# Top-32 selection on halves of the keys, and MLP work paced by the steps left

## The chip, the cores and the metric

The kernel runs on one core of a Trainium2 chip, in fp32. The metric is the device time of one execution in microseconds. PE is the matrix engine, DVE the vector engine, ACT the scalar engine, POOL is GpSimd, SP issues most of the DMAs.

## The reference

Attention over the 32 best keys, and then an MLP block on its output. Cut to what matters:

```python
# q, k, v: batch 8, heads 8, sequence 576, head_dim 64
scores = scale * np.matmul(q, k.transpose(0, 1, 3, 2))
kth = np.partition(scores, -32, axis=-1)[..., -32:-31]
scores = np.where(scores >= kth, scores, -1e9)
scores = scores - scores.max(-1, keepdims=True)
attn = np.exp(scores); attn = attn / (attn.sum(-1, keepdims=True) + 1e-9)
x = (attn @ v) as (8, 576, 512)                      # heads side by side
xn = (x - mean) / np.sqrt(var + 1e-6) * g_ln         # over the 512 columns
out = x + np.maximum(xn @ w_ch1, 0) @ w_ch2          # 512 -> 2048 -> 512
```

## The kernel before, in words

The work is cut into *units*. A whole unit is 128 queries of two heads (a head pair, `hp`); its scores are two tiles of 128 rows and 576 keys. The 64 queries that are left of each head pair form a *rest unit*: both heads in one tile. There are 160 units: 128 whole and 32 rest. Units are grouped into *jobs* (a batch, a head pair and some query tiles); batch 0 goes through query tiles 0 and 1 for all four head pairs, then 2 and 3, then the rests; later batches go through 0 and 1 and then 2 and 3, and the rests are added to the second part in batch 1 and to the first part from batch 2 on.

The main loop runs over steps n, and step n is named after the unit whose selection falls in it. Each engine works through its instructions in the order in which the loop emits them, so one step holds pieces of several units:

- PE and ACT: `scores(n+1)`, matmuls into PSUM (L347) and ACT copies of 288 columns into the tile `sc` (L328);
- DVE: `select(n, 0..3)` at four places of the step. It finds the 32nd largest score of each row: four times MAX8 (the eight largest of a row, L364), with three MATCH_REPLACE8 between them that overwrite these eight by a very low number (L369; each comes with a short MATCH_VALUE_LOAD). All of them run over 576 columns. The first reads `sc`, the others the scratch `wk`;
- ACT and POOL: `prepare(n-1)` computes the bias of the exponential (from unit 16 on POOL does, L390 and L391), `mask(n-1)` writes e from sc and the threshold (L394), and `weigh` takes the exponential of unit n-2 (L404);
- PE and ACT: `turn` transposes the weights of unit n-2 (L457, L490). For some whole units (`moved`, 84 in all) one tile goes another way instead: a DVE transpose (L434) and DMAs;
- PE: `values` multiplies a finished group of units with v (L515, L522), `place` transposes the output back (L554);
- DVE: `turn_heads` transposes k and q of a coming job (L300), `stats` computes mean and variance of finished rows (L581, L582), after which POOL subtracts the mean (L583).

In the first steps (up to 15) ACT, POOL and DVE also convert the 32 pieces of the weights w1 and w2, which arrive as 64-bit numbers (`weights`, L178 to L197).

The MLP runs on PE in the gaps. When two row tiles of a batch are finished (three where the rests of two batches are added), they become a `Block`; at a fixed step `give` puts its work into the list `todo`: transposes of x (L611), 64 `hidden` matmuls (L624) and 16 `project` matmuls a tile (L641). Blocks are given at steps 9, 19, 31, 44 (three tiles), 55, 63, 76 (three), 83, 95, 103, 116 (three), 123, 135, 143, 156 (three) and 163. `fill`, called at eight places of a step, takes items from `todo` as long as their costs are covered by what is `owed`; each call adds an eighth of what the planner allows the step (but no more than 6 us in all may be owed):

```python
DVE_UNIT, DVE_REST, DVE_MOVE = 10.3, 5.3, 0.8
def slot(n):
    return max(0.0, dve_cost(n) - pe_cost(n)) / SLOTS
```

`dve_cost` and `pe_cost` are the planner's own estimates for the step without MLP, in us. What remains in `todo` after the last step is run off at once.

In the code shown here, `halve` and what belongs to it are not yet there.

Of the kernel before, what the change touches and what calls it, by code (L numbers as in the profile page):

```python
# [10 lines left out]
ALU = mybir.AluOpType  # L11
FP32 = mybir.dt.float32
U32 = mybir.dt.uint32
PSUM = bass.MemoryType.PSUM

TOP_K = 32
LOWEST = -3.0e38
# [11 lines left out]
def kernel(  # L29
# [41 lines left out]
    nc = tc.nc  # L71
    P = nc.NUM_PARTITIONS
    B, H, S, D = q.shape
    DM = H * D
    DFF = w_ch2.shape[0]
    NC, NF = DM // P, DFF // P
# [8 lines left out]
    def pool(name, bufs, **kw):  # L85
        return ctx.enter_context(tc.tile_pool(name=name, bufs=bufs, **kw))
# [3 lines left out]
    HALF = S // 2  # L90
# [3 lines left out]
    kqpool = pool("kq", 4)  # L94
    vpool = pool("v", NV)
    scpool = pool("sc", 4)
    wpool = pool("wk", 2)
    epool = pool("e", 3)
    ptpool = pool("pt", 1)
    otpool = pool("ot", 2)  # L100
    restpool = pool("ot_rest", 1)
    small = pool("small", 4)
# [6 lines left out]
    hbmpool = pool("hbm", 4, space=bass.MemoryType.DRAM)  # L109
    psps = pool("ps", 5, space=PSUM)  # L110
    mmps = pool("mmps", 3, space=PSUM)

    def const(shape, name):
        return consts.tile(shape, FP32, tag=name, name=name)
# [20 lines left out]
    w2 = const([P, NF, DM], "w2")  # L135
# [4 lines left out]
    class Piece:  # L140
# [22 lines left out]
        def fetch(self):  # L163
            self.raw = xpool.tile([P, DM, 2], U32, tag="x", name="raw")
            nc.sync.dma_start(self.raw[:].rearrange("p n w -> p (n w)"), self.src)

        def split(self):
# [3 lines left out]
            high = self.raw[:, :, 1].bitcast(FP32)  # L171
            self.size = tmp("size", U32)
            self.low = tmp("low", FP32)
# [16 lines left out]
        def join(self):  # L190
            size = self.size[:]
            nc.gpsimd.tensor_tensor(size, size, self.low[:].bitcast(U32), ALU.add)
            size = size.bitcast(FP32)
# [42 lines left out]
    todo = []  # L236
    stores = []
    share = [0.0]
# [65 lines left out]
    class Unit:  # L304
        def __init__(self, job, group, qt):
            self.job, self.group, self.qt = job, group, qt
            self.rest = qt == J
            self.tiles = [(0, 1)] if self.rest else [(0,), (1,)]

            self.moved = False  # L310
            self.weighed = 0

    class Group:
# [18 lines left out]
    def score_half(u, s):  # L332
# [20 lines left out]
                    )  # L353
        return pss

    def select(u, i):

        nt = range(len(u.tiles))
        if i == 0:
            u.cur = [u.sc[:, t] for t in nt]  # L360
            u.wk = {}
        m = small.tile([P, 2, 8], FP32, tag=f"m{i}", name=f"m{i}")
        for t in nt:
            nc.vector.max(m[:, t, :], u.cur[t])  # L364
        if i < TOP_K // 8 - 1:
            for t in nt:
                if i == 0:
                    u.wk[t] = wpool.tile([P, S], FP32, tag="wk", name="wk")
                nc.vector.match_replace(u.wk[t][:], m[:, t, :], u.cur[t], LOWEST)  # L369
                u.cur[t] = u.wk[t][:]  # L370
        if i == 0:
            u.top = m
        u.thr = m
# [321 lines left out]
    units = []  # L695
# [8 lines left out]
    END = N + 6  # L704
# [9 lines left out]

    CONVERTING = max(n for n in batches if batches[n]) + 2
    EARLY = jobs[NHP].first
    for u in units[CONVERTING:]:
        u.moved = not u.rest and u is not u.group.units[-1]

# [2 lines left out]
    gives = {}  # L722
# [8 lines left out]
    for j in jobs:  # L731
        if j.hp == NHP - 1:
            b = j.b
            step = j.last + (3 if j.last < EARLY else 4)
            tiles = [(b, qt) for g in j.groups for qt in g.qts if qt < J]
# [17 lines left out]
    SLOTS = 8  # L753
# [4 lines left out]
    def after(n):  # L758

        turned = at(n - 1) if n - 1 < EARLY else at(n - 2) if n - 2 >= EARLY else None  # L760
        last = at(n - 2) if n - 2 < EARLY else at(n - 3) if n - 3 >= EARLY else None
        return turned, last.group if last and last is last.group.units[-1] else None

    DVE_UNIT, DVE_REST, DVE_MOVE = 10.3, 5.3, 0.8


    turns = {}
# [4 lines left out]
    def pe_cost(n):  # L772
        c = 0.0
        if at(n + 1):
            c += 1.25 if at(n + 1).rest else 1.5
        ex, g = after(n)
        if ex:
            c += 0.67 if ex.rest else 0.55 if ex.moved else 1.0
        if g:
            c += 0.6 + 7.8e-3 * g.nq  # L780
        return c

    def dve_cost(n):
        u, ex = at(n), after(n)[0]
        c = 5.0 if u is None else DVE_REST if u.rest else DVE_UNIT
        return c + DVE_MOVE if ex and ex.moved else c

    def give(n):
# [8 lines left out]

    def slot(n):

        return max(0.0, dve_cost(n) - pe_cost(n)) / SLOTS  # L800

    recips, rows_of = {}, {}

# [18 lines left out]
    for n in range(END):  # L822
        now[0] = n
        if n in gives:
            give(n)
        share[0] = slot(n)
        u, nxt, mk = at(n), at(n + 1), at(n - 1)
        ex, g = after(n)
        g = g if g and not g.quick else None
        late = at(n - 4)  # L830
        late = late if late and late.rest and late.job.b % 2 else None
        parts = turn(ex) if ex else []
        early = ex is not None and n - 1 < EARLY
        last = ex and ex is ex.group.units[-1]
        quick = ex.group if last and ex.group.quick else None

        moved = ex is not None and ex.moved
        order = (1, 0) if moved else (0, 1)
        sent, stores[:] = stores[:], []

        if ex and not early:
            weigh(ex, order[0])
        if nxt:
            scores(nxt)
        if g:
            values(g)
        if u:
            select(u, 0)
        if moved:
            move(ex)  # L850
        for store in sent:
            store()
        for den in recips.pop(n, []):
            nc.vector.reciprocal(den, den)
        if n == gives_first:
            for blk, i in rows_of.pop(n):
                blk.stats(i)
        if mk:
            prepare(mk)
        if early:  # L860
            for t in range(2):
                mask(ex, t)
                weigh(ex, t)
        if not quick:
            weights(n, 0)
        fill()
        if ex and len(ex.tiles) > 1 and not early:
            weigh(ex, order[1])
        fill()
        if parts and not moved:  # L870
            parts[0]()
        if ex and ex.rest:
            keep_den(ex)
        if u:
            select(u, 1)
        if n in turns:
            turn_heads(turns[n])
            later = fresh.index(turns[n]) + 1
            if later < len(fresh):
                load(fresh[later], nc.sync, nc.sync)  # L880
        for blk, i in rows_of.pop(n, []):
            blk.stats(i)
        for blk in gives.get(n - 1, []):
            blk.std()
        if not quick:
            weights(n, 1)
        fill()
        if mk and not early:
            mask(mk, int(mk.moved))
        if g:  # L890
            place(g)
        if late:
            place_rest(late.job.b, late.job.hp)
        fill(1 if g or late else 0)
        fill()
        if moved:
            parts[0]()
        elif len(parts) > 2:
            parts[1]()
        if u:  # L900
            select(u, 2)
        for blk in gives.get(n - 2, []):
            blk.inverse()
        if last and ex.group.sums is not None:
            recips.setdefault(n + 1, []).append(ex.group.sums)
        last_rest = at(n - 3)
        if last_rest and last_rest.rest and last_rest.job.b % 2:
            hp = last_rest.job.hp
            den = dr[last_rest.job.b // 2][:, 2 * hp : 2 * hp + 2]
            recips.setdefault(n + 1, []).append(den)  # L910
        fill()
        if parts:
            parts[-1]()
        if mk and len(mk.tiles) > 1 and not early:
            mask(mk, 1 - int(mk.moved))
        fill()
        for x in (u if n < EARLY else None, mk if n > EARLY else None):
            if x and x is units[x.job.last]:
                load_values(x.job)
        if quick:  # L920

            values(quick)
            for den in recips.pop(n + 1):
                nc.vector.reciprocal(den, den)
            place(quick)
            weights(n, 0)
            weights(n, 1)
        if u:
            select(u, 3)
        for x in (g, quick):  # L930
            if x and x.job.hp == NHP - 1:
                for qt in x.qts:
                    if qt < J:
                        arrived(n, (x.job.b, qt), xs[x.job.b, qt])
        if late and late.job.hp == NHP - 1:
            r = late.job.b // 2
            arrived(n, ("r", r), rs[r])
        fill()
# [37 lines left out]
```

## Time and profile before

| | |
|---|---|
| Median of 15 runs | 1751.93 us (1749.52 to 1755.8) |
| The profiled execution | 1750.6 us, of which its span is 1748.8 us |
| Mean granted PE clock | 0.962 of full speed |
| Busy time | PE 1616.1, DVE 1547.8, ACT 1117.1, POOL 287.7 us |
| Selection on DVE | MAX8 1152 instructions, 814.4 us; MATCH_REPLACE8 864 instructions, 635.7 us |
| MLP on PE | hidden 547.9 us, project 532.8 us of modelled busy time |
| Last unit's selection starts | 1612.1 us |

Busy time on PE is modelled: the records of matmuls that follow one another overlap, so their pitch, from start to start, tells more than their length. The same holds a little for DVE: a MAX8 record lasts 0.74 us, but the next one starts 0.66 us after it. In a row of the trace the first number is the start in us from the span's start, then comes the duration, the engine, the line, the operation, and the tiles written and read with their shapes; "x2" merges two instructions. A row of the groups ends with the busy time, the mean in ns of one, and the idle time of the engine before it with what ended it. In the page's slices each digit is a fortieth of the span, 43.7 us.

### The profile page before, as it was taken

To read this page: it belongs to the slowest core of one execution; us is meant where nothing else is said; L and a number is where in the kernel's file an instruction comes from. 1 tells how busy PE (TensorE), PEld (TensorE's weight loads), DVE (VectorE), ACT (ScalarE), POOL (GpSimd) and SP (SyncE) were. 2 spreads that over 40 slices of the span, in tenths; PEclk is the share of its full clock that TensorE was granted. 3 is DMA by queue.
4 is the path that set the end of the run, shared out by engine and by line. 5 is a ranking of instruction groups with operands and counts; after the bars stand their busy time and mean duration, and the time that the engine had idled before them with its cause. 6 is when DMAs were issued, how large, how long until landed. Compare 5 with 4: busy or idle time off the path is not lost.

```text
span 1748.8 us, 23687 instructions
## 1 busy us (share of the span) xinstructions
PE 1616.1 (92%) x7065; PEld 972.7 (56%) x7065; DVE 1547.8 (89%) x3228; ACT 1117.1 (64%) x2842; POOL 287.7 (16%) x513
## 2 busy tenths in 40 slices
PE   4559899799699999999999999999999999998998
PEld 2337466475355575745547575745547575745564
DVE  7987999989989999999999999999999999999100
ACT  7767876656565766666666676666656667667310
POOL 5664510010100101010110101010110101001000
PEclk9669999889799999999999999999999999999999
DMA  7432233112321133212322132212322132111000
GB/s 177 116 91 67 70 63 69 56 44 70 77 57 50 51 77 78 56 50 58 77 69 56 45 72 75 64 50 58 70 74 59 45 72 69 51 56 45 19 18 13
DMA packets 309832, 110.79 MB, mean 63 GB/s; under 512 B 247236, under 2 KB 290248, under 8 KB 309704
## 3 DMA queue, kind: packets, MB, share of 16 engines
q1 hardware_dynamic: 304968, 108.68, 24.4%
q10 hardware_dynamic: 4736, 0.59, 0.3%
q8 instruction: 57, 0.93, 0.2%
q14 instruction: 71, 0.58, 0.1%
HBM read 77.73 MB, written 31.46 MB: 62 GB/s over the span
## 4 chain that ended last, share of the span: by engine, by line
PE 69%; DVE 13%; ACT 8%; issue 7%; POOL 2%; DMA 1%; POOLq 0%; ACTq 0%; SPq 0%; DVEq 0%
PE hps L624 26%; PE ops L641 19%; PE scps L347 9%; PE av L515 7%; DVE m L364 6%; DVE wk L369 5%; PE tp L457 4%; PE av L522 2%; ACT e L404 2%; ACT e L394 1%; PE tp L611 1%; PE xo L554 1%; ACT size L178 1%; ACT sc L328 1%; POOL x L583 1%
## 5 line engine op out<-in xcount | busy, mean ns | idle before, releaser
L364 DVE MAX8 m<-wk 128x8 f32<-128x576 f32 x864 | 611.0, 744 | 2.0
L624 PE MATMUL hps<-xT,w 128*128 128x256 f32 (+1 forms) x2048 | 547.9, 414 | 6.5 <-ACT xT L616 4.0
L641 PE MATMUL ops<-w,h 128*128 128x512 f32 x1152 | 532.8, 596 | 0.0
L624 PEld LDWEIGHTS hps<-xT,w 128*128 128x128 f32 x2048 | 379.6, 193 | 111.9 <-issue 19.7
L369 DVE MATCH_REPLACE8 wk<-m,wk 128x576 f32<-128x576 f32 x576 | 423.8, 743 | 0.0
L641 PEld LDWEIGHTS ops<-w,h 128*128 128x128 f32 x1152 | 203.6, 190 | 196.5 <-issue 192.9
L347 PE MATMUL scps<-kT,qT 64*128 64x288 f32 (+3 forms) x1344 | 245.4, 444 | 32.0 <-DVE qT L300 14.7
L328 ACT COPY sc<-scps 128x288 f32<-128x288 f32 x576 | 197.8, 418 | 56.0 <-PE scps L347 42.3
L404 ACT ACTIVATE e<-e,bias 128x576 f32<-128x576 f32 x288 | 226.7, 787 | 0.8
L394 ACT ACTIVATE e<-sc,m 128x576 f32<-128x576 f32 x288 | 224.4, 779 | 1.6 <-DVE m L364 0.8
L347 PEld LDWEIGHTS scps<-kT,qT 64*128 64x128 f32 (+1 forms) x1344 | 136.6, 183 | 145.6 <-issue 49.2
L369 DVE MATCH_REPLACE8 wk<-m,sc 128x576 f32<-128x576 f32 x288 | 211.9, 743 | 0.0
L364 DVE MAX8 m<-sc 128x8 f32<-128x576 f32 x288 | 203.4, 743 | 6.9 <-ACT sc L328 6.9
L636 ACT ACTIVATE h<-hps 128x256 f32<-128x256 f32 (+1 forms) x256 | 105.5, 413 | 161.2 <-PE hps L624 159.7
L457 PE MATMUL tp<-ident,e 128*128 128x128 f32 x816 | 132.8, 288 | 47.9 <-ACT e L404 47.7
L457 PEld LDWEIGHTS tp<-ident,e 128*128 128x128 f32 x816 | 103.2, 147 | 121.7 <-ACT e L404 70.6
L390 POOL TENSOR_TENSOR bias<-m,m 128x2 f32<-128x2 f32 (+1 forms) x144 | 28.1, 195 | 832.2 <-DVE m L364 763.3
L515 PE MATMUL av<-pt,vb 128*64 128x256 f32 (+2 forms) x1088 | 149.8, 418 | 3.0 <-DMA vb<-in_v_dram 2.8
L515 PEld LDWEIGHTS av<-pt,vb 128*64 128x64 f32 x1088 | 75.1, 144 | 72.1 <-issue 24.7
L469 ACT COPY pt<-tp 128x512 f32<-128x512 f32 x128 | 75.5, 590 | 55.8 <-PE tp L457 55.3
L527 ACT COPY oT<-av 128x256 f32<-128x256 f32 (+2 forms) x68 | 26.3, 387 | 116.7 <-PE av L522 116.7
L434 DVE STREAM_TRANSPOSE sc<-e 128x512 f32<-128x512 f32 x84 | 59.3, 705 | 40.0 <-ACT e L404 40.0
(70 smaller groups left out, 1096.7 us busy)
## 6 DMA issues: line engine op xcount, KB each, us to landing
turned<-sc SPq DMA_DIRECT2D x84, 256.0 KB, 2.0
pt<-turned SPq DMA_DIRECT2D x336, 64.0 KB, 2.0
vb<-in_v_dram SPq DMA_DIRECT2D x136, 128.0 KB, 2.5
raw<-in_moe_w_ch_dram SPq DMA_DIRECT2D x32, 512.0 KB, 4.1
kin<-in_k_dram SPq DMA_DIRECT2D x128, 72.0 KB, 2.4
qin<-in_q_dram SPq DMA_DIRECT2D x120, 72.0 KB, 2.5
out_dram<-o SPq DMA_DIRECT2D x32, 256.0 KB, 2.2
ends<-in_v_dram SPq DMA_DIRECT2D x136, 16.0 KB, 2.3
```

The costliest lines, as they stand in the source:

```text
L328: nc.scalar.copy(u.sc[:, t, s * HALF : (s + 1) * HALF], made[s][t][:, 0:HALF])
L347: nc.tensor.matmul(ps[i * R : i * R + ql, o : o + width], qT[r, q0 : q0 + ql], kT[r, k0 : k0 + width], start=True, stop=True,)
L364: nc.vector.max(m[:, t, :], u.cur[t])
L369: nc.vector.match_replace(u.wk[t][:], m[:, t, :], u.cur[t], LOWEST)
L394: nc.scalar.activation(u.e[:, t], u.sc[:, t], AF.Prelu, bias=u.thr[:, t, 7:8], scale=-1.0, alpha=SLOPE)
L404: nc.scalar.activation(u.e[:, t], u.e[:, t], AF.Exp, bias=u.bias[:, t : t + 1], scale=-scale / SLOPE, accum_out=g.den[:, col : col + 1],)
L457: nc.tensor.transpose(ps[:, c * P : (c + 1) * P], u.e[:, t, c * P + t * R : (c + 1) * P + t * R], ident[:],)
L469: nc.scalar.copy(g.pt[:, 0:J, q0 : q0 + P], ps[:].rearrange("p (c n) -> p c n", n=P))
L515: nc.tensor.matmul(av[h * D : (h + 1) * D, 0 : g.nq], vb[:, h * J + c, :], g.ptB[:, 0 : g.nq // 32, c, :] if h else g.pt[:, c, 0 : g.nq], ...
L624: nc.tensor.matmul(ps["h"][:, 0:N], w1[:, c, f * P : (f + 1) * P], xT[0][:, c, 0:N], start=(c == 0), stop=(c == NC - 1),)
L636: nc.scalar.activation(hT[f], ps["h"][:, 0:N], AF.Relu)
L641: nc.tensor.matmul(ps["o"][:], hT[f][:, i * P : (i + 1) * P], w2[:, f, :], start=(f == 0), stop=(f == NF - 1),)
```

## The change

From unit 8 on (`EARLY`), the selection works on halves of the keys. The 576 scores of a row are taken as 288 pairs (column j with column 288 + j). DVE writes the larger of each pair into a new tile `hi`. GpSimd computes the smaller one from the bits, as integers: it adds both scores into `lo` and, once `hi` is there, subtracts it, which leaves exactly the other one's bits. At most 16 of the 32 largest scores can be smaller ones of their pair. So `select_halved` takes the 16 largest of `lo` (two MAX8 and one MATCH_REPLACE8 over 288 columns) and writes them into 16 columns behind the 288 of `hi`; then the four MAX8 and three MATCH_REPLACE8 follow over the 304 columns of `hi`. `halve(n+1)` is emitted in step n after `select(n, 1)`.

The first 8 units keep the old selection; their scratch is now the last part of the tile `w2`, which isn't filled yet at that time. The pool `wk` goes; `hi` (two buffers), `lo` (one) come in its place, and the pool `e` has two buffers instead of three.

In the planner a halved unit's cost on DVE counts 0.9 of what it did. After step 16 a step is allowed the larger of two: the old difference of DVE and PE costs, and the cost of all that is in `todo` divided by the number of steps to the next block plus two.

```diff
-    wpool = pool("wk", 2)
-    epool = pool("e", 3)
+    hipool = pool("hi", 2)
+    lopool = pool("lo", 1)
+    epool = pool("e", 2)
...
+    def halve(u):
+        nt = len(u.tiles)
+        u.lo = lopool.tile([P, 2, HALF], FP32, tag="lo", name="lo")
+        u.hi = hipool.tile([P, 2, HALF + TOP_K // 2], FP32, tag="hi", name="hi")
+        a, b = u.sc[:, 0:nt, 0:HALF], u.sc[:, 0:nt, HALF:S]
+        lo, hi = u.lo[:, 0:nt], u.hi[:, 0:nt, 0:HALF]
+        nc.gpsimd.tensor_tensor(lo.bitcast(I32), a.bitcast(I32), b.bitcast(I32), ALU.add)
+        nc.vector.tensor_tensor(hi, a, b, ALU.max)
+        nc.gpsimd.tensor_tensor(
+            lo.bitcast(I32), lo.bitcast(I32), hi.bitcast(I32), ALU.subtract
+        )
+
+    def select_halved(u, i):
+        nt = range(len(u.tiles))
+        def replace(m, t, x):
+            nc.vector.match_replace(x[:, t], m[:, t, :], x[:, t], LOWEST)
+        if i == 0:
+            for o in range(HALF, HALF + TOP_K // 2, 8):
+                for t in nt:
+                    nc.vector.max(u.hi[:, t, o : o + 8], u.lo[:, t])
+                if o == HALF:
+                    for t in nt:
+                        replace(u.hi[:, :, o : o + 8], t, u.lo)
+            return
+        for r in ((0,), (1,), (2, 3))[i - 1]:
+            m = small.tile([P, 2, 8], FP32, tag=f"m{r}", name=f"m{r}")
+            for t in nt:
+                nc.vector.max(m[:, t, :], u.hi[:, t])
+            if r < TOP_K // 8 - 1:
+                for t in nt:
+                    replace(m, t, u.hi)
+            if r == 0:
+                u.top = m
+            u.thr = m
+
     def select(u, i):
+        if u.halved:
+            return select_halved(u, i)
...
-                    u.wk[t] = wpool.tile([P, S], FP32, tag="wk", name="wk")
-                nc.vector.match_replace(u.wk[t][:], m[:, t, :], u.cur[t], LOWEST)
-                u.cur[t] = u.wk[t][:]
+                    o = (NF - 4 + 2 * t) * DM
+                    u.wk[t] = w2[:].rearrange("p f n -> p (f n)")[:, o : o + S]
+                nc.vector.match_replace(u.wk[t], m[:, t, :], u.cur[t], LOWEST)
+                u.cur[t] = u.wk[t]
...
+    for u in units[EARLY:]:
+        u.halved = True
...
-    DVE_UNIT, DVE_REST, DVE_MOVE = 10.3, 5.3, 0.8
+    DVE_UNIT, DVE_REST, DVE_HALVED, DVE_MOVE = 10.3, 5.3, 0.9, 0.8
...
+        if u and u.halved:
+            c *= DVE_HALVED
...
     def slot(n):
-        return max(0.0, dve_cost(n) - pe_cost(n)) / SLOTS
+        share = max(0.0, dve_cost(n) - pe_cost(n))
+        if n > CONVERTING:
+            new = min((x for x in gives if x > n), default=END - 2)
+            share = max(share, sum(t[1] for t in todo) / (new + 2 - n))
+        return share / SLOTS
...
         if u:
             select(u, 1)
+        if nxt and nxt.halved:
+            halve(nxt)
```

More of the change, by code (lines that the diff above doesn't have):

```diff
@@ L13 @@
 U32 = mybir.dt.uint32
+I32 = mybir.dt.int32
 PSUM = bass.MemoryType.PSUM
@@ L310, in __init__ @@
             self.moved = False
+            self.halved = False
             self.weighed = 0
```

## The prediction

> **What bounds the kernel now.** I read the page first: busy times, then the slices.
>
> ```profile
> span 1748.8 us, 23687 instructions
> ...
> PE 1616.1 (92%) x7065; PEld 972.7 (56%) x7065; DVE 1547.8 (89%) x3228; ACT 1117.1 (64%) x2842; POOL 287.7 (16%) x513
> ...
> PE   4559899799699999999999999999999999998998
> ...
> DVE  7987999989989999999999999999999999999100
> ...
> PEclk9669999889799999999999999999999999999999
> ```
>
> PE and DVE are both near full from about 500 us on, DVE stops at about 1622 us, and PE goes on alone to the end: a tail of 127 us. Before 250 us PE is half idle, its granted clock down to 0.6 in some slices, because MLP work isn't there yet. So DVE and PE must be weighed stretch by stretch. The table by windows (PE, PEld, DVE, ACT, POOL busy) gives 40 steps (two batches, units 80 to 119) and the tail:
>
> ```profile
> 831.00:1227.00 396.00, 387.86 (x1738) 233.56 (x1737) 384.81 (x803) 262.96 (x671) 43.83 (x106) 1.00 0.25 63
> 1622.00:1749.00 127.00, 119.93 (x398) 68.47 (x397) 2.75 (x8) 25.05 (x59) 9.84 (x9) 1.00 0.06 17
> ```
>
> DVE is 97% busy and PE 98%: neither can get much shorter without meeting the other. DVE's timeline shows a whole unit:
>
> ```profile
> 1017.13 1.40 DVE L364 MAX8 m<-sc 128x8 f32<-128x576 f32 x2
> 1018.45 0.07 DVE L369 MATCH_VALUE_LOAD wk<-m,sc 128x8 f32 x1
> 1018.51 0.74 DVE L369 MATCH_REPLACE8 wk<-m,sc 128x576 f32<-128x576 f32 x1
> ...
> 1026.77 0.75 DVE L364 MAX8 m<-sc 128x8 f32<-128x576 f32 x1
> ```
> ```profile
> 1163.41 0.14 DVE L854 RECIPROCAL den<-den 128x4 f32<-128x4 f32 x1
> 1163.46 0.73 DVE L364 MAX8 m<-wk 128x8 f32<-128x576 f32 x1
> ```
>
> From start to start a unit takes 9.64 us: 8 MAX8 at 0.66 and 6 replacements at 0.73 (0.07 of it the value load). A 4-column instruction takes 0.05 from start to start. So I split 0.66 into 0.06 fixed and 0.60 for 576 columns, 1.04 ns a column. A rest unit (one tile, each instruction waiting for the one before, 0.11 each) takes 5.49. The starts of the first MAX8 of each unit are the step starts; most steps last exactly what their DVE instructions add up to.
>
> PE's pitch is read in the tail, where nothing disturbs it:
>
> ```profile
> 1687.80 27.79 PE L624 MATMUL hps<-xT,w 128*128 128x256 f32 x128
> 1715.43 27.63 PE L641 MATMUL ops<-w,h 128*128 128x512 f32 x64
> ```
>
> A block of two row tiles costs 27.6 + 27.6 us and 0.44 a tile for its transposes: 56.1; one of three 84.2. Attention costs PE 128.4 us per 40 steps (scores 1.17 a whole unit, values 2.95 or 2.41 a group, turns 0.54 to 0.97, 0.6 of pause a group); a group of values with 320 columns reads so:
>
> ```profile
> 1162.31 2.37 PE L515 MATMUL av<-pt,vb 128*64 128x320 f32 x16
> 1164.61 0.81 PE L522 MATMUL av<-pt,ends 128*128 128x320 f32 x2
> 1165.26 2.74 PE L641 MATMUL ops<-w,h 128*128 128x512 f32 x6
> ```
>
> With 9 tiles of MLP (252.7) that is 381. DVE's sum for the same steps: 32 x 9.64, 8 x 5.49, 24 moves at 0.66, 8 pairs of head transposes at 1.33, 9 stats at 0.84, 2.4 of small ones: 388.8, against 396 measured.
>
> **The change, part by part.** *DVE, whole unit.* On the halves: 4 MAX8 of 288 columns at 0.36 and 2 replacements at 0.42 (2.28); 8 MAX8 of 304 at 0.376 and 6 replacements at 0.44 (5.65); the elementwise maximum of 2 x 288 at 0.68 (no such row; the 576-column replacement at 0.66 and transpose at 0.69 are nearest). Sum 8.61, or 1.03 less. The two tiles still alternate, so I take no waits between dependent instructions; if half of the 0.11 appeared on all 20, 1.1 would be added and the gain gone. *Rest unit.* 1.14 + 2.82 + 0.38, and ten waits of 0.11: 5.4, no gain.
>
> *GpSimd.* Two integer instructions per unit. The rows:
>
> ```profile
> L192 POOL TENSOR_TENSOR size<-size,low 128x512 uint32<-128x512 uint32 x32 | 41.2, 1288 | 3.1 <-DVE size L186 3.1
> L390 POOL TENSOR_TENSOR bias<-m,m 128x2 f32<-128x2 f32 x112 | 22.0, 197 | 745.4 <-DVE m L364 682.4 <-ACT e L394 31.6 <-ACT sc L328 20.3
> ```
>
> give 2.14 ns a column: 1.43 us for 576. Per 40 steps 104 us join 44, in 396: not a bound. In order of one step, the sum can start when ACT's copies of the next scores end (about 3 us after the step's start, 0 to 5.5 in steps 80 to 119) and the one `lo` buffer is free (after the new select 0, at 2.3). DVE's maximum is due at 3.95 us, 4.6 with a move. The difference then has the 4 us of selects 2 and 3 as cover, and 2.3 of it are left; behind it on POOL wait the centring of x (1.58 us a tile) and o's additions, which are needed a step later. *New waits.* DVE's maximum now waits mid-step for copies that were needed only at the next step; behind it are the head transposes, stats and selects 2 and 3. While DVE is the bound the copies are there; while PE is, DVE has time. I add 0.15 per whole unit and 0.1 per rest unit, for the steps without a move in which the sum, begun at 3.1, would still be running at 3.95.
>
> The rule that speaks against this is in the Trainium skill, "SBUF — State Buffer", section "Who interferes with whom": a VectorE instruction with two SBUF inputs and a GpSimd one that reads SBUF exclude each other for the whole instruction. No run here shows it, since no VectorE instruction of before reads two tensors. By that rule a maximum that is due just after the sum has begun waits up to its whole length, and the total would be that of the slower rival below; with engines that don't disturb each other, as the trace's POOL and DVE rows run side by side, it is that of the forecast.
>
> *Buffers.* One e buffer less: e lives from its mask in step n+1 to its last turn in n+2, so two suffice; without that cover ACT would wait for a turn at the end of a step. Scratch in w2 serves units 0 to 7, before its pieces arrive: nothing.
>
> *Pacing.* No instruction changes, only when PE's MLP comes. The old term (DVE less PE cost) shrinks by about 1 us a whole step with DVE_HALVED; the new one asks for the queue's cost over the steps to the next block plus two. In the 7 steps from 76, with a queue that was empty, 84.2 over 7 + 2 steps leave about two ninths (17) at the end: 67.0 us of MLP run, where the old term (44.5 in all, and what was owed) let 48.8 through.
>
> *The sum.* For each stretch between blocks I take the larger of PE's and DVE's sums, before -> after. As an example steps 103-116: DVE 10 whole units, 3 rest units, 8 moves, 2 head pairs, 3 stats and 0.8 of small ones, 124.1 -> 115.3; PE 38.1 of attention and 75.1 -> 62.2 of MLP (all that is queued), 113.2 -> 100.3: DVE is last. Steps 19-31: DVE 117.1 -> 108.3. 31-44: DVE 122.0 -> 114.1. 44-55 (three tiles): PE 107.2 -> 113.3. 55-63: 80.4 -> PE 78.4. 63-76: DVE 124.1 -> 115.3. Then twice the four stretches of two batches: 76-83 (three tiles in 7 steps, attention 26.1) PE 75.0 -> 93.1; 83-95 PE 113.7 -> 109.3 (attention 35.9); 95-103 80.4 -> 78.4; 103-116 DVE 124.1 -> 115.3. 156-160: PE 48.0 -> 53.2. The sum is 1385.1 before, where the step starts show 1394.8 (0.7% off), and 1374.8 after: -10.3. After the last unit PE has 113.3 -> 108.2 left: -5.1. So two batches in the steady state even lose 3: what DVE saves in one stretch is spent where PE is full, and work run early leaves PE without MLP in steps 113 to 115. Steps 0 to 18 I count at nothing (±4): in 8 to 13 copies on ACT end 7 to 16 us into the step, so DVE isn't last there. Together -15.4.
>
> The profiled execution took 1750.6 (span 1748.8 and 1.8 around it), 1.3 below the median of 1751.93. So 1735 for a profiled execution, 1737 for the median. The measurement tells about 0.2% (3.5 us) from no change.
>
> **The rivals.** *Slower: the maximum waits for GpSimd.* Place: DVE mid-step, when copies arrive after 2.5 us. For: copies at 3 to 5 us in most steps, so both instructions become ready together. Against: POOL is idle and may be done first. In the stretches where DVE is last, some 50 whole units lie, so 0.1 us more per unit costs 5 us; from 9.1 us on 83-95 and 95-103 join, and it costs 9. At 9.03 us a unit the gain is used up (0.42 of waiting); at 9.3 the sums give +27 - 5, 1774; with a full 1.43 on every unit +103 - 5, 1850. I take 1774.
>
> *No change: coupling eats it.* Scores are now due some 5 us earlier in the step, so PE and DVE can drift apart less. Summing the larger one per step instead of per stretch gives 1426 after; before, the measured 1394.8 lay 30% of the way from stretches (1385) to steps (1419). Half way after would be near 1400, 6 above the measured 1394.8, less 5 in the tail: 1753.
>
> *Much faster: the pace keeps PE fed.* PE's sums alone from step 44 on, and DVE's only in 19-44, give some 1335: 50 less than before, and 5 in the tail: 1697. Against: the old larger-of-two term stays, and empties the queue in long stretches.
>
> **How the numbers follow.** Forecast (1715 to 1748 by itself: from no allowance and PE sums 3% high, as 75.0 against the 72.9 measured in steps 76 to 83, to break-even) 0.43; much faster 0.07; no change 0.12; waiting on GpSimd 0.38. So faster 0.50, same 0.12, slower 0.38. The range 1702 to 1784 takes in up to 0.8 us of waiting per unit (9.4: +38 - 5) and reaches most of the way to the fastest case; longer waits, and the fastest case's lower half, are what is left out.
>
> **What would show it.** Right: a whole unit's DVE instructions sum to 8.5 to 8.9 us; the new POOL rows are near 1.4 us; DVE is idle before its maximum mostly in the 7-step stretches, waiting for ACT's copies; PE idles before blocks 95 and 116; the tail is shorter by about 5 us. Wrong: the maximum's row far above 0.75 us or idle time before it put down to POOL; select 0 waiting for the difference; steps 76 to 83 not some 15 us longer than 72.9; unit sums above 9.1.

## The result, and the profile after

The changed kernel takes 1758.84 us (1757.62 to 1760.55) against 1753.06, the median of all 53 runs of the kernel before: a ratio of 1.0037 with a 95% interval of 1.0028 to 1.0047. It is slower by a little, and clear of noise. The profiled execution has a span of 1757.3 us, 8.5 more than before. The page's first lines:

```profile
span 1757.3 us, 25335 instructions
...
PE 1615.0 (92%) x7065; PEld 972.8 (55%) x7065; DVE 1454.2 (83%) x4468; ACT 1119.8 (64%) x2842; POOL 685.1 (39%) x817
...
PE   4658899899699999979999999989999999988998
...
DVE  7986889979988989996798999997689999998100
```

DVE has 94 us less to do, as intended, and PE the same as before; the time didn't follow. What is new is that DVE's slices show holes (6 and 7) at slices 19 and 20 and at 28 and 29, which is where steps 76 to 83 and 116 to 123 lie. The page's groups of the new instructions (busy, mean ns, idle before and its releaser):

```profile
L372 POOL TENSOR_TENSOR lo<-sc 128x576 int32<-128x576 int32 (+1 forms) x152 | 204.6, 1346 | 392.4 <-ACT sc L332 288.6
L374 POOL TENSOR_TENSOR lo<-lo,hi 128x576 int32<-128x576 int32 (+1 forms) x152 | 195.0, 1283 | 115.0 <-DVE hi L373 111.2
L387 DVE MAX8 hi<-lo 128x8 f32<-128x288 f32 x544 | 222.1, 444 | 20.2 <-POOL lo L374 19.1
L373 DVE TENSOR_TENSOR hi<-sc 128x576 f32<-128x576 f32 (+1 forms) x152 | 133.4, 878 | 45.2 <-ACT sc L332 45.2
L485 DVE STREAM_TRANSPOSE sc<-e 128x512 f32<-128x512 f32 x84 | 59.0, 703 | 103.3 <-ACT e L455 103.2
```

DVE seldom stands idle for GpSimd (19 us in the whole run; some 27 more lie inside the maximum's own records, see e8). It waits for ACT: 45 us before the maximum and 103 us before the transposes of `move`, where it waited 40 before:

```profile
L434 DVE STREAM_TRANSPOSE sc<-e 128x512 f32<-128x512 f32 x84 | 59.3, 705 | 40.0 <-ACT e L404 40.0
```

ACT isn't full (64%); it stands in the order of the program behind PE's results. DVE's timeline of a whole unit shows the cost that was forecast (8.61):

```profile
1024.46 0.81 DVE L387 MAX8 hi<-lo 128x8 f32<-128x288 f32 x2
...
1033.10 0.80 DVE L387 MAX8 hi<-lo 128x8 f32<-128x288 f32 x2
```

From start to start 8.64 us against 9.64. So the selection did get faster by a tenth, and the loss lies in *when* PE works. The timeline of step 82, a rest step, shows it: 6.15 us long before, 16.2 now (849.5 to 865.7).

```profile
850.53 0.46 DVE L387 MAX8 hi<-lo 128x8 f32<-128x288 f32 x1
851.08 0.60 PE L508 MATMUL tp<-ident,e 128*128 128x128 f32 x4
851.51 1.02 PE L692 MATMUL ops<-w,h 128*128 128x512 f32 x2
851.71 0.59 ACT L524 COPY pt<-tp 128x512 f32<-128x512 f32 x1 [3.47 <-PE tp L508]
852.48 2.74 PE L692 MATMUL ops<-w,h 128*128 128x512 f32 x6
...
853.52 0.76 ACT L455 ACTIVATE e<-e,bias 128x576 f32<-128x576 f32 x1
...
854.41 0.71 DVE L485 STREAM_TRANSPOSE sc<-e 128x512 f32<-128x512 f32 x1 [3.41 <-ACT e L455]
...
861.51 1.27 POOL L705 TENSOR_TENSOR o<-o,x 128x512 f32<-128x512 f32 x1 [11.35 <-ACT o L701]
862.74 1.40 POOL L372 TENSOR_TENSOR lo<-sc 128x576 int32<-128x576 int32 x1
...
864.22 1.40 POOL L374 TENSOR_TENSOR lo<-lo,hi 128x576 int32<-128x576 int32 x1
...
865.66 0.46 DVE L387 MAX8 hi<-lo 128x8 f32<-128x288 f32 x1 [4.88 <-POOL lo L374]
```

DVE has finished the first part of a short selection and then stands 3.41 us, because PE is still at MLP matmuls (L692) of the step before; ACT copies PE's turned weights first (it waited 3.47 us for them), then takes the exponential, and only then may DVE transpose. The longest stop, 4.88 us, ends the step: the next unit's `lo` comes late, because GpSimd's sum stands behind an addition of the MLP (L705) that waited 11.35 us for ACT's result, and that for PE's projections. So in such a step PE's lateness reaches DVE through GpSimd too. The table by windows for this one step (PE, PEld, DVE, ACT, POOL busy; after, then before):

```profile
849.50:865.70 16.20, 16.20 (x65) 8.05 (x64) 6.32 (x19) 7.29 (x19) 4.52 (x6) 1.00 0.10 33
```

```profile
852.40:858.50 6.10, 5.64 (x37) 3.13 (x36) 5.93 (x14) 3.85 (x11) 0.41 (x2) 1.00 0.19 62
```

PE is busy through all 16.2 us, DVE for 6.3 of them. Before, both fitted a step of 6.1.

The step starts (the first MAX8 of each unit on DVE) divide the whole span. "Three-tile stretches" are steps 44-54, 76-82 and 116-122, each after a block of three tiles; rest steps are those from 20 on. For the runs described below the same sums stand beside it. All in us of the profiled executions:

| | before | after | no pacing (e1) | pacing only (e2) | paced whole steps (e5) | paced rest steps (e6) |
|---|---|---|---|---|---|---|
| steps 0 to 19 | 234.1 | 239.0 | 239.8 | 236.8 | 239.3 | 239.2 |
| 28 rest steps | 184.4 | 244.9 | 190.7 | 219.6 | 212.1 | 215.5 |
| 20 whole steps in three-tile stretches | 220.8 | 236.8 | 190.9 | 243.7 | 227.5 | 212.6 |
| 91 other whole steps | 972.8 | 903.5 | 866.4 | 1008.1 | 904.2 | 937.4 |
| from the start of the last unit | 136.7 | 133.1 | 221.4 | 132.8 | 133.6 | 137.1 |
| span | 1748.8 | 1757.3 | 1709.1 | 1840.9 | 1716.7 | 1741.8 |
| DVE idle in the 28 rest steps | 16.3 | 58.8 | 15.8 | 50.1 | 34.1 | 31.7 |
| PE idle in the 28 rest steps | 13.7 | 3.4 | 9.9 | 6.1 | 11.3 | 3.4 |
| PE idle in the 91 other whole steps | 29.3 | 48.9 | 14.7 | 97.2 | 16.8 | 36.6 |

After against before: 69 us gained in the other whole steps, 60 lost in the rest steps, 16 in the three-tile stretches, 5 at the beginning, and 3.6 gained at the end. The last three rows, by the modelled busy time for PE, show how: in the rest steps PE is busy for nearly all of the 245 us while DVE stands 59, and in the other whole steps PE stands 49 us, where e1 needs 15.

### The profile page after: what moved, and what is told of

Same layout as the page of the kernel before. It is cut to its first block, busy times and chain, and to the rows that moved or that the text cites. A ratio compares the mean times of both kernels' runs of the same rounds, so it can differ in the third digit from the quotient of the medians.

```text
span 1757.3 us, 25335 instructions
## 1 busy us (share of the span) xinstructions
PE 1615.0 (92%) x7065; PEld 972.8 (55%) x7065; DVE 1454.2 (83%) x4468; ACT 1119.8 (64%) x2842; POOL 685.1 (39%) x817
## 4 chain that ended last, share of the span: by engine, by line
PE 62%; DVE 22%; ACT 6%; issue 4%; POOL 4%; DMA 1%; SPq 0%; POOLq 0%; DVEq 0%; ACTq 0%
PE hps L675 26%; PE ops L692 18%; PE scps L351 6%; DVE m L395 6%; DVE hi L382 5%; PE av L566 5%; PE tp L508 3%; DVE hi L387 3%; DVE hi L373 2%; DVE lo L382 2%; PE av L573 2%; ACT e L455 1%; POOL x L634 1%; DVE sc L485 1%; ACT e L445 1%
## 5 line engine op out<-in xcount | busy, mean ns | idle before, releaser
L692 PE MATMUL ops<-w,h 128*128 128x512 f32 x1152 | 537.7, 597 | 2.8 <-POOL w L199 2.8
L395 DVE MAX8 m<-hi 128x8 f32<-128x304 f32 x1088 | 460.4, 458 | 2.1
L382 DVE MATCH_REPLACE8 hi<-m,hi 128x304 f32<-128x304 f32 x816 | 368.1, 456 | 0.0
L372 POOL TENSOR_TENSOR lo<-sc 128x576 int32<-128x576 int32 (+1 forms) x152 | 204.6, 1346 | 392.4 <-ACT sc L332 288.6
L692 PEld LDWEIGHTS ops<-w,h 128*128 128x128 f32 x1152 | 202.9, 191 | 191.2 <-issue 182.1
L351 PE MATMUL scps<-kT,qT 64*128 64x288 f32 (+3 forms) x1344 | 239.0, 447 | 31.3 <-DVE qT L302 14.6
L374 POOL TENSOR_TENSOR lo<-lo,hi 128x576 int32<-128x576 int32 (+1 forms) x152 | 195.0, 1283 | 115.0 <-DVE hi L373 111.2
L387 DVE MAX8 hi<-lo 128x8 f32<-128x288 f32 x544 | 222.1, 444 | 20.2 <-POOL lo L374 19.1
L351 PEld LDWEIGHTS scps<-kT,qT 64*128 64x128 f32 (+1 forms) x1344 | 132.8, 185 | 144.6 <-issue 52.3
L373 DVE TENSOR_TENSOR hi<-sc 128x576 f32<-128x576 f32 (+1 forms) x152 | 133.4, 878 | 45.2 <-ACT sc L332 45.2
```

The costliest lines, as they stand in the source:

```text
L351: nc.tensor.matmul(ps[i * R : i * R + ql, o : o + width], qT[r, q0 : q0 + ql], kT[r, k0 : k0 + width], start=True, stop=True,)
L372: nc.gpsimd.tensor_tensor(lo.bitcast(I32), a.bitcast(I32), b.bitcast(I32), ALU.add)
L382: nc.vector.match_replace(x[:, t], m[:, t, :], x[:, t], LOWEST)
L387: nc.vector.max(u.hi[:, t, o : o + 8], u.lo[:, t])
L395: nc.vector.max(m[:, t, :], u.hi[:, t])
L692: nc.tensor.matmul(ps["o"][:], hT[f][:, i * P : (i + 1) * P], w2[:, f, :], start=(f == 0), stop=(f == NF - 1),)
```

## The experiments

Two theories: P, that the pacing costs the time and the selection on halves pays; H, that the selection on halves costs it, by its hand-overs between the engines.

**e1, no pacing.** The three lines of pacing go; the selection on halves stays.

```diff
-        if n > CONVERTING:
-            new = min((x for x in gives if x > n), default=END - 2)
-            share = max(share, sum(t[1] for t in todo) / (new + 2 - n))
```

> The changed kernel with the old allowance per step (difference of DVE and PE costs alone, halved units at 0.9); the selection on halves stays. Theory P (the pacing by number of steps puts as much MLP into a short rest step and into the 7-step stretches as PE can't run beside DVE's work, so steps there last as long as PE; the selection itself pays): steps 76 to 83 near 66 us instead of 91, rest steps back near 6.2 to 6.5 us, DVE's selection ends some 90 us earlier, but the tail grows to about 210 us because too little MLP is let through; in all about 1738 us (1725 to 1750), some 20 below the changed kernel. Theory H (the selection on halves itself costs the time, by hand-overs between DVE, ACT and GpSimd): no better than the changed kernel, 1758 or more.

Measured: 1711.13 us, ratio 0.9765 (0.9751 to 0.978). Theory P, and by more than it expected (1725 to 1750). Steps 76 to 83 took 63.2 us instead of 91.4, and the last unit started 136 us earlier, for 88 us more behind it. The page:

```profile
span 1709.1 us, 25338 instructions
...
PE 1604.0 (94%) x7065; PEld 967.0 (57%) x7065; DVE 1434.9 (84%) x4468; ACT 1116.0 (65%) x2842; POOL 679.1 (40%) x817
...
PE   4668899999799999999999999999999999999998
...
DVE  7986989989989999999999999999999999900000
```

From slice 12 on PE's digit is 9 to the last but one, and from slice 13 on DVE's too until its selection ends, 136 us earlier than after. Five slices of PE alone look like waste and aren't: PE is full there, with MLP that isn't pressed into steps too short for it. DVE's waits (engine, line, waited for: us, times, longest) in this run:

```profile
DVE hi L373 <- ACT sc L332: 19.9, 8, 9.0
DVE sc L485 <- ACT e L455: 15.2, 7, 7.3
```

The 103 us before `move` have shrunk to 15.

**e2, pacing alone,** in the kernel before (selection over 576 keys, old buffers).

```diff
-        return max(0.0, dve_cost(n) - pe_cost(n)) / SLOTS
+        share = max(0.0, dve_cost(n) - pe_cost(n))
+        if n > CONVERTING:
+            new = min((x for x in gives if x > n), default=END - 2)
+            share = max(share, sum(t[1] for t in todo) / (new + 2 - n))
+        return share / SLOTS
```

> The kernel before with the new allowance alone (the larger of the old one and the queue over the steps left plus two); selection over 576 keys, old buffers. Theory P: rest steps and the 7-step stretches get longer here too, with no faster DVE to pay for it: about 1824 us (1790 to 1850), and steps 76 to 83 near 90 us. Theory H: the pacing is neutral or a small gain, within 10 us of before.

Measured: 1840.36, ratio 1.0498 (1.0476 to 1.052). The pacing alone costs 89 us; steps 76 to 83 took 84.3, a little less than expected. The engines' line of the page, and the wait that marks the pacing here too (40 us before):

```profile
PE 1650.1 (90%) x7065; PEld 994.6 (54%) x7065; DVE 1550.3 (84%) x3228; ACT 1117.9 (61%) x2842; POOL 287.3 (16%) x513
```

```profile
DVE sc L434 <- ACT e L404: 135.6, 55, 7.7
```

So the change has two parts of opposite sign, which don't add: the halves by themselves bring -41 us, the pacing by itself costs +89, and both together make +6, not +48. On top of the halves the pacing costs less (48), because the tail that it saves there is longer: from e1 to after the steps take 136 us more and the tail 88 less; from before to e2, 96 more and 4 less.

PE's busy time counts the same 7065 matmuls in each run and still differs: 1604.0 us in e1, 1615.0 after, 1650.1 in e2, at a mean granted clock of 0.968, 0.955 and 0.934. In steps 76 to 82 that clock is 1.00 in e1 and 0.93 after. So of the 48 us between e1 and after, 37 are PE standing idle and 11 are PE being busy for longer. In these runs the lower clock goes along with more idle time on PE; no run tells the two apart.

**e3, the smaller by DVE.** The two GpSimd instructions are replaced by a minimum on DVE.

```diff
-        nc.gpsimd.tensor_tensor(lo.bitcast(I32), a.bitcast(I32), b.bitcast(I32), ALU.add)
         nc.vector.tensor_tensor(hi, a, b, ALU.max)
-        nc.gpsimd.tensor_tensor(lo.bitcast(I32), lo.bitcast(I32), hi.bitcast(I32), ALU.subtract)
+        nc.vector.tensor_tensor(lo, a, b, ALU.min)
```

> The changed kernel with the smaller of each pair taken by a second DVE instruction (elementwise minimum) instead of the two on GpSimd: no shared access of the two engines and no wait for GpSimd, but 0.66 us more on DVE per whole unit. Theory P: DVE's sum per whole unit 9.30 against 8.64 and 0.24 of measured waiting, so slower by about 30 us, near 1785 (1770 to 1800). Theory H: the hand-over was the cost, so the same or faster than the changed kernel, 1740 to 1760. In both the maximum's row falls to about 0.75 us.

Measured: 1783.08, ratio 1.0177 (1.0161 to 1.0194), where theory P put it. GpSimd's part is worth its hand-overs even in the changed kernel.

**e4, no pacing and a higher planned cost.** As e1, and a halved unit counts 0.95 instead of 0.9, so that whole steps let more MLP through.

```diff
-    DVE_UNIT, DVE_REST, DVE_HALVED, DVE_MOVE = 10.3, 5.3, 0.9, 0.8
+    DVE_UNIT, DVE_REST, DVE_HALVED, DVE_MOVE = 10.3, 5.3, 0.95, 0.8
```

> The selection on halves with the old allowance per step, and a halved unit counted at 0.95 instead of 0.9, so that each whole step lets about 0.5 us more MLP through. Theory P: PE and DVE sums meet in nearly every stretch and the tail is about 155 us: near 1709 us (1690 to 1735), faster than both kernels. Theory H: 1755 or more. If 0.95 lets more through than PE can run, the steps grow instead and it is no faster than with 0.9.

Measured: 1712.48, ratio 0.9776 (0.9761 to 0.9791), within 0.1% of e1: the last unit starts 51 us later and the tail is 50 us shorter (171.6 against 221.4). With PE full, it matters little where in the order its MLP stands, as long as the steps can hide it.

**e5 and e6, which steps.** The pacing on whole steps only, and on rest steps only.

```diff
-        if n > CONVERTING:
+        if n > CONVERTING and not (at(n) and at(n).rest):     # e5
+        if n > CONVERTING and at(n) and at(n).rest:           # e6
```

> The changed kernel with the pacing by steps on whole steps only; a rest step is allowed the old difference again. Theory R (most of the pacing's cost comes from rest steps, which last 6 us on DVE and are given as much MLP as a whole step of 9): rest steps back to about 195 us in the 28 rest steps from 20 on, against 244.9, and in all near 1715 us (1700 to 1730). Theory D (the cost comes from the stretches of 7 steps with a three-tile block, where PE is full): 1740 to 1758.

> The mirror of it: the pacing by steps on rest steps only, whole steps with the old difference. Theory R: near 1745 us (1735 to 1758). Theory D: near 1720 us, because the whole steps of the 7-step stretches are no longer filled.

Measured: e5 1718.31, ratio 0.9804 (0.9781 to 0.9826); e6 1743.67, ratio 0.9949 (0.993 to 0.9968). Against e1 the pacing costs 7 us on whole steps and 33 on rest steps; together 48. Most of it comes from the rest steps. Theory R's totals hold for both, its way there only in part: in e5 the rest steps came to 212.1 and not to 195, since some of them still inherit PE's lateness from the whole step before (step 82 took 12.4 us, against 16.2 after and 6.2 in e1). The three-tile stretches of e5 are nearly as long as after (86.3 us for steps 76 to 83), and still cost little in the end: against e1 the steps of e5 take 95 us more and the tail 88 less, and PE stands idle for 109 us in all against 105.

**e7, paced by time.** The queue is shared out by the planned DVE time of the steps left, not by their number.

```diff
-            share = max(share, sum(t[1] for t in todo) / (new + 2 - n))
+            left = sum(dve_cost(x) for x in range(n, new)) + 2 * DVE_HALVED * DVE_UNIT
+            share = max(share, sum(t[1] for t in todo) * dve_cost(n) / left)
```

> The changed kernel with the queue shared out by DVE's planned time instead of by the number of steps: a step gets the queue's cost times its own DVE cost over that of the steps left plus two whole ones. Rest steps get about 0.55 of a whole step's share. Theory R: near 1730 us (1715 to 1740), between the version without pacing and the changed kernel. Theory D: 1745 or more, since the 7-step stretches stay as full as they were (steps 76 to 83 near 90 us in both theories).

Measured: 1739.43, ratio 0.9923 (0.9904 to 0.9942), at the upper end of theory R's range: better than by number, worse than none. DVE's time isn't the right measure either. Probably it is because a rest step has its own attention on PE too, so that the room beside it is less than DVE's time suggests; that is argued, not shown.

**e8, GpSimd behind the maximum.** The same two integer instructions in another order, so that none of them runs beside the maximum.

```diff
-        nc.gpsimd.tensor_tensor(lo.bitcast(I32), a.bitcast(I32), b.bitcast(I32), ALU.add)
         nc.vector.tensor_tensor(hi, a, b, ALU.max)
-        nc.gpsimd.tensor_tensor(lo.bitcast(I32), lo.bitcast(I32), hi.bitcast(I32), ALU.subtract)
+        nc.gpsimd.tensor_tensor(lo.bitcast(I32), a.bitcast(I32), hi.bitcast(I32), ALU.subtract)
+        nc.gpsimd.tensor_tensor(lo.bitcast(I32), lo.bitcast(I32), b.bitcast(I32), ALU.add)
```

> The changed kernel with both GpSimd instructions behind DVE's maximum (first score minus larger, then plus the other score, the same integers): neither reads while the maximum runs. If the two engines exclude each other, the maximum's mean falls from 989 ns to about 760, with some left from the centring of x. Theory P (DVE isn't last where the waiting happens): the total stays within 8 us of the changed kernel, or grows by up to 8 because the difference is ready 1.4 us later. Theory H (the waiting of the maximum decides): 27 us of DVE time saved show in the total, 1730 to 1740.

Measured: 1766.24, ratio 1.0076 (1.0055 to 1.0096). The groups by shape, after and e8:

```profile
L373 DVE TENSOR_TENSOR hi<-sc 128x576 f32<-128x576 f32 x120 | 118.6, 989 | 38.0 <-ACT sc L332 38.0
```

```profile
L372 DVE TENSOR_TENSOR hi<-sc 128x576 f32<-128x576 f32 x120 | 91.6, 763 | 41.9 <-ACT sc L332 41.8
```

The maximum falls from 989 to 763 ns: in the changed kernel it does wait inside its own record for GpSimd's sum. But 27 us less on DVE bring nothing; the total grows by 7.4, and DVE's wait for `lo`, which is ready later in this order, from 19 to 31 us. So that waiting is real and doesn't decide here. What it costs without the pacing wasn't measured by itself.

**e9, two e buffers** in the kernel before (`epool = pool("e", 2)`).

> The kernel before with two e buffers instead of three, nothing else. All theories: within 0.3% of before, near 1752 us. If ACT's mask had to wait for the last turn of the unit two before, the steps would lengthen and the total would grow by 0.5% or more; then part of the changed kernel's loss would be the buffers'.

Measured: 1754.15, ratio 1.0005 (0.9992 to 1.0019). In the kernel before, the third buffer is worth nothing.

**e10, no pacing, the smaller by DVE:** e1 and e3 together.

> Selection on halves without the pacing, and the smaller of each pair by a second DVE instruction instead of the two on GpSimd. DVE's whole unit is then 9.30 us against 8.64 and some 0.13 of waiting, and without the pacing most steps last as long as DVE's instructions: 120 whole units by 0.53 us would be up to 60 us more than without the pacing (1711), near 1755 (1735 to 1775), if DVE is last there. If PE were last instead, or GpSimd's hand-over cost as much as it saves, it stays near 1711 to 1725.

Measured: 1776.18, ratio 1.0129 (1.0111 to 1.0146), just above the range: 65 us more than e1. Without GpSimd's part the selection on halves is slower than the old one. The same exchange cost 24 us in the paced kernel and 65 here; that fits PE being last in many steps there and DVE here.

## Why the prediction was wrong

It said faster, 1737, and the kernel is slower by 6 us; the sign is that of the other side. That the time lies inside the range is luck: the range reaches so far up for the sake of DVE waiting for GpSimd, and that isn't what cost the time.

*DVE's cost* was right: 8.64 us a unit against 8.61 in the steps shown. The allowance of 0.15 for GpSimd's sum was too small (0.24 as a mean over the units: 989 against about 750 ns), but e8 shows that this isn't where the total was lost. The rival that was to make it slower, DVE waiting for GpSimd, therefore gave the right sign for a wrong reason. *GpSimd* was right too: 1483 and 1413 ns for 576 columns, where 1.43 us was worked out. The rule of the Trainium skill ("SBUF — State Buffer", "Who interferes with whom") that a VectorE instruction with two SBUF inputs and a reading GpSimd one exclude each other agrees with the trace: the record grew from 0.75 us to at most 1.90.

*The sum* is the step that failed. For each stretch between blocks it took the larger of PE's and DVE's sums, as if the engines could drift apart over a whole stretch. From step 19 to the end of the last selection it forecast 10.3 us less than before; measured were 6.7 more (1394.8 to 1401.5). Steps 76 to 83, where PE's sum is the larger, came out close: put at 93.1, they took 91.4 and, 40 steps later, 90.7. Even there the parts were off: counted at the tail's pitch, 60.4 us of MLP ran and not 67.0, and PE stood 4.7 and 5.4 us. Where DVE's sum is the larger and rest steps alternate with whole ones, it failed: 31-44 took 124.4 (forecast 114.1; 7 of these 10 us were there before the change), 63-76 125.2 (115.3), 103-116 122.5 and 122.4 (115.3): 34 us in all. In the last three neither engine is full; PE stands 5.7 to 7.6 us and DVE 6.0 to 8.6. In 83-95 PE's sum was too small: PE was busy throughout, 115.9 us twice (109.3), 13 us in all, with 78.9 us of MLP where 73.4 were forecast, because steps 76 to 83 had let less through. The other stretches were forecast 21 us too long together. So the sums lie 27 us below the measured steps; before, they lay 10 below; 17 are the miss in the difference.

Most of the loss lies in the rest steps. They ran 4 us of MLP on the average, counted at the tail's pitch, and up to 11, and with that they last as long as PE: 245 us for the 28, with PE busy for 241.5 of them, where e1 shows 191 to be enough. The whole steps around them last about as long as DVE; neither pays for the other, because DVE can't run ahead of `move`, which waits for ACT's exponential, and that for PE. The second rival, "coupling eats it", named this kind of loss, by step instead of by stretch, and its 6 us for the steps from 19 on came near the 6.7. Its reason was another one, scores that are due earlier in the step; e2 shows that the pacing alone brings the loss, with the old selection. The rival had 0.12, while the stretches had fitted to 0.7% before, where both engines' work was matched step by step. That check was no test of a plan that unmatches them. And of the signs that were to show the forecast right, the unit's sum, the POOL rows and the length of steps 76 to 83 came true; none of them looked at the rest steps, where 60 us were lost.

The second thing missed was to price the two halves of the change apart. The forecast never asked what the halves bring without the pacing; e1 shows 88 us more of tail for 136 us less of steps. That needed no run: by the same sums, old allowance and new selection, the question could have been asked.

*The early steps*, 0 to 18, were put at ±4 and lost 3.8: step 7 takes 15.5 us where it took 11.2, with 3.7 us of DVE idle for the first `lo`, whose instructions stand behind the conversion of weights on POOL. *The tail* was put at 5.1 us shorter; from the end of the last selection it is 1.9 shorter (126.9 to 125.0). *The buffers* were put at nothing, which e9 shows for e in the kernel before.

The expectation for e1 erred the other way, by 27 us: it put the end of DVE's selection 90 us earlier, and it came 136 earlier. Without the pacing the loads are matched again, and the stretches' sums hold: 63-76 took 115.3 and 103-116 took 116.0, where DVE's sum of the forecast is 115.3. Left open is whether a pacing that knows PE's room in each step would beat e1; it wasn't tried.

The fastest version is e1: the selection on halves as changed, and the allowance per step as before, at 1711 us.

## What to carry to other kernels

Two engines that alternate in short steps can be summed over a stretch only if each step's loads match: when work is spread over steps, give each step what fits beside its own load on the other engine, not an equal share. A long tail in which one engine runs alone is no loss if that engine is the bound and full; work pulled out of it must be hidden somewhere, or it costs more than it saves. And a change of two parts should be priced as two, each with and without the other: here the halves bring 41 us without the pacing and 82 with it.

## What the runs showed of the hardware

A DVE maximum of two SBUF tensors (2 x 288 columns) takes 0.75 us with no GpSimd instruction beside it. Whichever engine starts first holds up the other. In 48 of the 120 whole units GpSimd's sum was running and the maximum took longer than 0.85 us, up to 1.90; each of these ended 0.61 to 0.62 us after the sum did. In 16 units the maximum had begun first, mostly by 0.05 us, and the sum took 1.92 to 1.98 us instead of 1.41. With both GpSimd instructions ordered behind it, the maximum's mean is 763 ns instead of 989. GpSimd's integer instructions on 576 columns take 1.41 us when nothing holds them up, nearly twice what DVE needs for the minimum (0.77). The Trainium skill ("GPSIMD Engine Reference", "Engine selection") advises VectorE for such work for that reason. The ratio agrees roughly (1.8 here); the advice doesn't hold here, because VectorE is last: moved to it, the minimum costs 65 us in all without the pacing and 24 with it.
